# The gate half of an attention + gated MLP kernel: w_in's 512 columns read from two halves in turn

## Chip, cores and metric

The kernel runs on one core of one Trainium2 chip. The metric is the device time of one execution in microseconds (us); lower is better. Three runs of the kernel before gave 534.77, 535.20 and 535.42 us.

## What is computed

Attention with pooled keys and values feeds a gated MLP with a spatial gate. Cut to what matters:

```python
# attention: 8 batches, 8 heads, 576 positions, 64 wide; K and V averaged in groups of 8
x = softmax(q @ pool(k).T / 8) @ pool(v)         # (8, 576, 512)
h = gelu_tanh(x @ w_in)                          # w_in (512, 1024)
u, v = h[..., :512], h[..., 512:]                # v: the gate half
v_n = (v - mean(v)) / sqrt(var(v) + 1e-6) * g_ln
v_s = w_sg @ v_n + b_sg                          # over the 576 positions
out = x + (u * v_s) @ w_out                      # w_out (512, 512)
```

## The kernel before

Everything stays on the chip between the loads and the stores. Each batch passes through steps with one-letter names: loads of K, V and q (A, B, C, E), pooling (K, P), scores and softmax (S), moving the probabilities to the layout of the next product (L, T), the product with V (V), the gate half of w_in's product (H), the other half (U), the spatial gate (W), the last product (O) and the store (Z). For batch 0 alone the products of H for the first four position tiles stand in a step of their own, J, which goes through the contraction chunks as w_in arrives; D fills TensorE at the start. The order of all steps over all batches is one long table written out by hand, `ORDER`; a dependency chain at the end of the program keeps each engine in that order. Batches overlap: steps of batch b+1 and b+2 stand between those of batch b.

Products in 32 bits that must be exact are done as three products in the type fp32r: an operand is split into a high part that fp32r holds and the rest, and high x high, high x rest and rest x high are summed in PSUM. `wih` and `wil` are the two parts of w_in, 128 partitions by 4 contraction chunks by 1024 columns; columns 512 to 1023 (`DF2:2 * DF2`) are the gate half. `xhl` holds the two parts of x, and `xta` the last 64 positions of both.

Step H works by tiles of 128 positions, five to a batch (the last has 64). For a tile, x is the stationary operand (`lhsT`) and the 512 gate columns of one chunk are the moving operand (`rhs`): 4 chunks x 3 products for each full tile; in the last tile high and rest of x stand side by side as one stationary operand, 4 chunks x 2 products. That is 4 x 12 + 8 = 56 products of 512 columns for a batch, 448 for eight. All of them are issued by the helper `mm` in line 140. The result goes through Gelu (L668), its mean and variance (L672, L673), and the normalisation (L484 or L488), in which a position's 512 columns are read as one row, and is split again (`vhh`, `vhl`, `vht`) for step W, in which the columns pick the rows of the output: d-th group of 128 columns for the d-th part of u. So the columns must leave H in their order.

The other products have moving operands of 288 columns (half of 576 positions: steps U, W, O, V) or 144 (the scores, S, in plain 32 bits).

w_in is loaded as it lies in memory (`load_w`, four loads of 1 MB, in a 64-bit type) and made into `wih` and `wil` by `step_w`: L276 and L279 on ScalarE (ACT) take the upper and the lower word of each 64-bit value, words that lie 8 bytes apart in `raw`; L278 and L281 put them together, and L220/L222 and L225 split them. Sums of eight neighbours on GpSimd (POOL) are in `sum8`: L360 adds the first and second half of each group of eight, then of each four; L361 adds elements 0 and 1 of each group, which lie 32 bytes apart from group to group.

Of the kernel before, what the change touches and what calls it, by code (L numbers as in the profile page):

```python
# [95 lines left out]
def tile_pooled_attn_gmlp(ctx: ExitStack, tc: tile.TileContext, q, k0, kv0, v0, k, v, vleft, w_in, w_sg, bg, w_out, out):  # L96
# [5 lines left out]
    DF2 = w_in.shape[1] // 2  # L102
# [3 lines left out]
    KC = DM // P  # L106
# [21 lines left out]
    def ring(pool, shape, name, bufs):  # L128

        turns[name] = (turns.get(name, -1) + 1) % bufs  # L130
        return pool.tile(shape, F32, name=name, tag=f"{name}{turns[name]}")

    def mtile():
        return ring(psm, [P, 2, NB], "mps", 2)

    def atile():
        return ring(psa, [P, 2, NB], "aps", 2)

    def mm(o, lhsT, rhs, start, stop):
        nc.tensor.matmul(o, lhsT, rhs, start=start, stop=stop)  # L140
# [49 lines left out]
    wih = const.tile([P, KC, 2 * DF2], F32R, name="wih")  # L190
    wil = const.tile([P, KC, 2 * DF2], F32R, name="wil")
# [7 lines left out]
    both = const.tile([P, S + DF2 // P], F32, name="both")  # L199
# [6 lines left out]
    def ready(func):  # L206

        if loaded.get("now") != func:
            nc.scalar.activation(early, eps[:, 0:1], func)
        loaded["now"] = func  # L210

    def copy(o, i, key):
        if key in OTHER:
            nc.vector.tensor_copy(o, i)
        else:
            nc.scalar.copy(o, i)  # L216
# [7 lines left out]
    def combine(o, x, y, op, key):  # L224
        (nc.vector if key in OTHER else nc.gpsimd).tensor_tensor(o, x, y, op=op)  # L225
# [112 lines left out]
    def step_D(b, _):  # L338

        for _ in range(DRY):  # L340
            ps = atile()[:, 0, 0:P]
            for _ in range(2):
                mm(ps, ident, ident, True, True)
            yield
# [131 lines left out]
    def root(rstd, var, key):  # L476
        n = rstd.shape[0]
        nc.gpsimd.tensor_tensor(rstd, var, eps[:n, 1:2], op=ALU.add)  # L478
        nc.gpsimd.tensor_tensor(rstd, rstd, mhalf[:n], op=ALU.pow)

    def scaled(vg, mv, rstd, key):

        if key in OTHER:
            nc.vector.scalar_tensor_tensor(vg, vg, mv[:, 0:1], rstd.broadcast_to(list(vg.shape)),  # L484
                                           op0=ALU.subtract, op1=ALU.mult)
            return
        nc.gpsimd.tensor_scalar(mv[:, 0:1], mv[:, 0:1], rstd, -1.0, op0=ALU.mult, op1=ALU.mult)
        nc.scalar.activation(vg, vg, AF.Identity, bias=mv[:, 0:1], scale=rstd)  # L488

    def step_S(b, g):  # L490
        qT = st.pop(("qT", b, g))
        flat = (mtile() if (b, g) in BY_M else atile()).rearrange("p a n -> p (a n)")
        slots = []
        for i in range(NT):
# [63 lines left out]
    def step_T(b, g):  # L558
        ef = st.pop(("e", b, g))
        tags = (("ah", "al"), ("lt0", "lt1"))[g % 2]  # L560
        if b == 0:
            st["a", b, g] = []
            for h in range(2):
                ps = atile().rearrange("p a n -> p (a n)")
                turn(ps, lambda i: ef[:, i, SP * h:SP * h + SP])
                yield
                t = per.tile([SP, S], F32, name=tags[h], tag=tags[h])
                copy(t, ps[0:SP, 0:S], f"T{h}{g}")
                st["a", b, g].append(t)
                yield  # L570
            return
# [49 lines left out]
    def step_J(b, c):  # L621

        xhl = st["xhl", b][0]
        if c == 0:
            st["hp"] = [t[:, i] for t in (mtile(), mtile()) for i in range(2)]
        for pairs in (((wih, 0), (wih, 1)), ((wil, 0),)):
            for i, o in enumerate(st["hp"]):
                t = slice(i * P, i * P + P)
                for w, x in pairs:
                    mm(o, xhl[:, x, c, t], w[:, c, DF2:2 * DF2], c == 0 and w is wih and x == 0, c == KC - 1 and w is wil)  # L630
            yield

    def step_H(b, i):
        by_c = b == 0 and i < NT - 1
        if by_c:
            yield
        xhl, xta = st["xhl", b]
        xhi, xlo = xhl[:, 0], xhl[:, 1]
        o = st["hp"][i] if by_c else mtile()[:, 0]
        n = min(P, S - i * P)  # L640
        t = slice(i * P, i * P + n)
        sl = slice(DF2, 2 * DF2)
        for c in range(0 if by_c else KC):
            if i < NT - 1:
                mm(o, xhi[:, c, t], wih[:, c, sl], c == 0, False)
                mm(o, xhi[:, c, t], wil[:, c, sl], False, False)
                mm(o, xlo[:, c, t], wih[:, c, sl], False, c == KC - 1)
            else:

                both = (xta[:, c].rearrange("p a t -> p (a t)"), wih[:, c, sl], c == 0, c == KC - 1)  # L650
                if c == 0:
                    mm(o, *both)
                mm(o[:n], xta[:, c, 0], wil[:, c, sl], False, False)
                if c > 0:
                    mm(o, *both)
        if not by_c:
            yield
        vg = ring(per, [P, DF2], "vg", 3)[:n]
        if i == NT - 1:
            nc.scalar.copy(vg, o[n:2 * n])  # L660
            yield
            nc.vector.tensor_tensor(vg, o[:n], vg, op=ALU.add)
            yield
            ready(AF.Gelu_apprx_tanh)
            nc.scalar.activation(vg, vg, AF.Gelu_apprx_tanh)
        else:
            ready(AF.Gelu_apprx_tanh)
            nc.scalar.activation(vg, o, AF.Gelu_apprx_tanh)  # L668
        yield
        bst = per.tile([P, 6], F32, name="bst", tag=f"bst{i}")[:n]  # L670
        mv = per.tile([P, 2], F32, name="mv", tag=f"mv{i}")[:n]
        nc.vector.bn_stats(bst, vg)  # L672
        nc.vector.bn_aggr(mv, bst)  # L673
        rstd = per.tile([P, 1], F32, name="rstd", tag=f"rstd{i}")[:n]
        root(rstd, mv[:, 1:2], f"r{min(b, 3)}{i}")
        yield
        scaled(vg, mv, rstd, f"z{min(b, 3)}{i}")
        yield
        if ("vh", b) not in st:
            st["vh", b] = (per.tile([P, NT - 1, DF2], F32R, name="vhh", tag="vhhi"),  # L680
                           per.tile([P, NT - 1, DF2], F32R, name="vhl", tag="vhlo"),
                           per.tile([P, DF2], F32R, name="vht"))
        vhh, vhl, vht = st["vh", b]
        hi, lo = (vhh[:, i], vhl[:, i]) if i < NT - 1 else (vht[0:TAIL], vht[TAIL:2 * TAIL])
        copy(hi, vg, f"g{min(b, 2)}{i}")
        yield
        if i < NT - 1:
            combine(lo, vg, hi.bitcast(F32), ALU.subtract, f"H{min(b, 2)}{i}")
        else:
            nc.vector.tensor_tensor(lo, vg, hi.bitcast(F32), op=ALU.subtract)  # L690
# [127 lines left out]
def _laid_out(inputs):  # L818

    import numpy as np  # L820

    a = {n: np.asarray(x) for n, x in inputs.items()}
    B, H, S, D = a["q"].shape
    G, SP, NT = H // 2, S // POOL, -(-S // P)
    q = a["q"].reshape(B, G, 2, S, D).transpose(0, 1, 2, 4, 3).reshape(B, G, 2 * D, S)
    at = [128 * min(r, 2) + 160 * max(r - 2, 0) + 32 * i + j
          for i in range(NT) for r in range(2 * (i == NT - 1), 4) for j in range(32)]
    a["q"] = np.stack([q[b] if b == 0 else q[b][:, :, at] for b in range(B)])
    n = P * (S // P)
    run = [t for lo, hi in ((0, 384), (448, 576), (384, 448)) for t in range(lo, hi)]  # L830
    kt = a["k"][0].reshape(G, 2, S, D).transpose(2, 0, 1, 3).reshape(S, G, 2 * D)[run]
    vt = a["v"][0].reshape(G, 2, S, D).transpose(2, 1, 0, 3).reshape(S, H * D)[run]
    a["k0"] = kt[:n].reshape(S // P, P, G, 2 * D).transpose(1, 2, 0, 3)
    a["v0"] = vt[:n].reshape(S // P, P, H * D).transpose(1, 0, 2)
    a["kv0"] = np.concatenate([kt[n:].reshape(S - n, H * D), vt[n:]])
    a["k"] = a["k"][1:].reshape(B - 1, G, 2, SP, POOL, D).transpose(0, 2, 5, 1, 3, 4).reshape(B - 1, 2 * D, G, SP, POOL)
    v = a["v"][1:].reshape(B - 1, G, 2 * SP, POOL, D).transpose(0, 1, 2, 4, 3)
    a["v"] = v[:, :, 0:P].transpose(0, 2, 1, 3, 4)
    a["vleft"] = v[:, :, P:].reshape(B - 1, G * (2 * SP - P), D, POOL)
    a["moe_w_sg"] = np.concatenate([a["moe_w_sg"].T, a["moe_w_sg"].T[n:]])  # L840
    a["bg"] = np.concatenate([np.broadcast_to(a["moe_b_sg"], (P, S)), a["moe_g_ln"].reshape(-1, P).T], axis=1)
    return a
# [21 lines left out]
```

## Time and profile before

| | |
|---|---|
| median of three runs | 535.2 us (534.77 to 535.42) |
| profiled execution, span from the first to the last instruction | 534.0 us |
| TensorE (PE) busy | 525.2 us, 98% of the span |
| weight loads of TensorE (PEld) busy, beside PE | 489.6 us |
| VectorE (DVE) / ScalarE (ACT) / GpSimd (POOL) busy | 376.9 / 257.9 / 240.5 us |
| mean granted TensorE clock | 0.999 of 2.4 GHz |

Of the profiled execution only its span is given; the runs are timed apart from it, and their median lies 1.2 us above that span. Busy time of PE counts overlapping matmuls once. A matmul's own duration, from its start to its modelled end, is longer than the distance to the next one, since they are pipelined; what a matmul takes of the span is read from the distance of starts, for which the chain of work that ended last is the best view: it gives stretches with their number of matmuls.

### The profile page before, as it was taken

Reading aid. Unit: us, or ns where it says so; the run is one execution under the profiler, and the core shown is the slowest. Engines: PE = TensorE matmul, PEld = TensorE weight load, DVE = VectorE, ACT = ScalarE, POOL = GpSimd, SP = SyncE. Lnnn points to the kernel's source line nnn. Section 1 sums busy time; section 2 is a strip of 40 time slices with the busy share of each in tenths; the row PEclk is TensorE's granted clock in tenths of the full one; section 3 lists DMA queues with packets and bytes.
Section 4 is the critical chain, followed back from the end, with each engine's and each line's share of the span. In section 5 each row is a group of like instructions: output and inputs, shape, how many; then the busy total and the mean of one; then the engine's idle time right before and its main releaser. Section 6 shows DMA issues by size and latency. Waiting matters only on the chain.

```text
span 534.0 us, 9508 instructions
## 1 busy us (share of the span) xinstructions
PE 525.2 (98%) x3594; PEld 489.6 (92%) x3594; DVE 376.9 (71%) x593; ACT 257.9 (48%) x510; POOL 240.5 (45%) x333
## 2 busy tenths in 40 slices
PE   8889999999999999999999999999999999999997
PEld 8658999889989999898998999989999999999997
DVE  1788999668857886876679769877749765642362
ACT  2787871586336554475613567274253743142100
POOL 4797664553445628173325614754134641251010
PEclk9999999999999999999999999999999999999999
DMA  8995125837461563056432533344431224000002
GB/s 284 405 335 187 54 68 127 241 101 231 103 182 57 151 222 96 24 144 201 129 106 87 181 89 87 112 108 117 139 126 23 88 68 112 24 22 23 23 2 110
DMA packets 42810, 66.64 MB, mean 125 GB/s; under 512 B 5532, under 2 KB 22028, under 8 KB 42764
## 3 DMA queue, kind: packets, MB, share of 16 engines
q1 hardware_dynamic: 42476, 65.59, 40.3%
q8 instruction: 28, 0.46, 0.4%
q10 hardware_dynamic: 288, 0.44, 0.2%
q14 instruction: 18, 0.15, 0.1%
HBM read 47.14 MB, written 18.73 MB: 123 GB/s over the span
## 4 chain that ended last, share of the span: by engine, by line
PE 96%; ACT 2%; DVE 1%; POOL 0%; issue 0%; POOLq 0%; ACTq 0%
PE mps L140 80%; PE aps L140 15%; ACT e L469 1%; PE aps L187 0%; DVE nmax L503 0%; ACT ah L216 0%; ACT vg L668 0%; ACT xhl L216 0%; ACT raw L279 0%; ACT x L216 0%; DVE e L460 0%; ACT vg L488 0%; DVE bst L672 0%; DVE vhl L225 0%; ACT top L276 0%
## 5 line engine op out<-in xcount | busy, mean ns | idle before, releaser
L140 PE MATMUL mps<-xhl,wih 128*128 128x288 f32 x512 | 88.7, 294 | 0.1
L140 PE MATMUL mps<-wih,xhl 128*128 128x512 f32 x256 | 82.0, 398 | 0.0
L140 PEld LDWEIGHTS mps<-xhl,wih 128*128 128x128 f32 x512 | 75.2, 188 | 1.3 <-ACT vht L216 0.4
L455 POOL TENSOR_TENSOR e<-e,ssum 128x720 f32<-128x720 f32 x29 | 42.1, 1455 | 58.0 <-DVE ssum L454 53.5
L140 PEld LDWEIGHTS mps<-wih,xhl 128*128 128x128 f32 x256 | 47.8, 188 | 10.7
L232 POOL TENSOR_TENSOR xhl<-x,xhl 128x576 fp32r<-128x576 f32 x22 | 31.3, 1433 | 53.9 <-ACT x L216 34.6
L140 PE MATMUL mps<-wsh,vhh 128*128 128x288 f32 x256 | 54.8, 295 | 0.0
L140 PE MATMUL mps<-wsl,vhh 128*128 128x288 f32 x256 | 54.7, 295 | 0.0
L140 PE MATMUL mps<-wsh,vhl 128*128 128x288 f32 x256 | 54.7, 295 | 0.0
L140 PE MATMUL mps<-xhl,wil 128*128 128x288 f32 x256 | 54.6, 294 | 0.0
L140 PE MATMUL mps<-ghi,woh 128*128 128x288 f32 x244 | 53.1, 298 | 0.0
L140 PE MATMUL mps<-glo,woh 128*128 128x288 f32 x244 | 52.3, 294 | 0.0
L140 PE MATMUL mps<-ghi,wol 128*128 128x288 f32 x244 | 52.3, 294 | 0.0
L722 DVE SCALAR_TENSOR_TENSOR mps<-mps,both 128x576 f32<-128x576 f32 x32 | 26.1, 814 | 34.9 <-PE mps L140 34.6
L140 PE MATMUL mps<-wil,xhl 128*128 128x512 f32 x128 | 48.6, 395 | 0.0
L478 POOL TENSOR_TENSOR rstd<-mv,eps 128x1 f32<-128x1 f32 (+1 forms) x40 | 9.9, 247 | 80.3 <-DVE mv L673 79.9
L225 POOL TENSOR_TENSOR glo<-u,ghi 128x576 fp32r<-128x576 f32 x18 | 25.7, 1430 | 41.0 <-ACT ghi L216 23.9
L140 PEld LDWEIGHTS aps<-kbd,qT 128*128 128x128 f32 x300 | 39.0, 190 | 4.5 <-ACT ah L216 1.4
L140 PE MATMUL aps<-kbd,qT 128*128 128x144 f32 x300 | 41.6, 288 | 1.5 <-ACT ah L216 1.2
L760 DVE TENSOR_TENSOR x<-mps,x 128x576 f32<-128x576 f32 x30 | 22.4, 745 | 27.3 <-PE mps L140 27.2
L140 PEld LDWEIGHTS mps<-wsh,vhh 128*128 128x128 f32 x256 | 41.1, 188 | 0.4 <-issue 0.4
L140 PEld LDWEIGHTS mps<-wsh,vhl 128*128 128x128 f32 x256 | 41.1, 188 | 0.2 <-DVE vhl L225 0.2
(182 smaller groups left out, 1256.7 us busy)
## 6 DMA issues: line engine op xcount, KB each, us to landing
qT<-in_q SPq DMA_DIRECT2D x31, 288.0 KB
out<-x SPq DMA_DIRECT2D x31, 288.0 KB
kraw<-in_k SPq DMA_DIRECT2D x14, 576.0 KB
vraw<-in_v SPq DMA_DIRECT2D x14, 512.0 KB
al<-tfar SPq DMA_DIRECT2D x20, 288.0 KB
tfar<-y SPq DMA_DIRECT2D x56, 80.0 KB
raw<-in_moe_w_in SPq DMA_DIRECT2D x4, 1024.0 KB
tfar<-y SPq DMA_DIRECT2D x56, 64.0 KB
```

The lines of the kernel that those rows point to most:

```text
L140: nc.tensor.matmul(o, lhsT, rhs, start=start, stop=stop)
L225: (nc.vector if key in OTHER else nc.gpsimd).tensor_tensor(o, x, y, op=op)
L232: nc.gpsimd.tensor_tensor(lo, x, hi, op=ALU.subtract)
L455: (nc.gpsimd if key in OTHER else nc.vector).tensor_tensor(e, e, rec.unsqueeze(3).broadcast_to([P, NT, 2, SP]), op=ALU.mult)
L469: nc.scalar.activation(e[:, i, h], slots[i][:, h], AF.Exp, bias=nmax[:, i, h:h + 1], accum_out=ssum[:, i, h:h + 1])
L478: nc.gpsimd.tensor_tensor(rstd, var, eps[:n, 1:2], op=ALU.add)
L722: nc.vector.scalar_tensor_tensor(vs, vs, gcol[:, d:d + 1], bbc.rearrange("p (a n) -> p a n", a=2), op0=ALU.mult, op1=ALU.add)
L760: nc.vector.tensor_tensor(x, ps[:, :, 0:HALF], x, op=ALU.add)
```

## The change

The moving operand of every gate-half product is read by an access pattern that takes column 0 of the slice, column 256, column 1, column 257, and so on: 256 pairs whose two elements lie 256 columns (1024 bytes) apart. On the host the gate half of w_in is set out so that the even columns come first and the odd ones after them; read in that way, they come out in order. Loads, splits, number of products, number of columns and the order of issue on all engines are the same as before.

```diff
+    def woven(x):
+        return x.rearrange("p (a b) -> p b a", a=2)
+
...
                 for w, x in pairs:
-                    mm(o, xhl[:, x, c, t], w[:, c, DF2:2 * DF2], c == 0 and w is wih and x == 0, c == KC - 1 and w is wil)
+                    mm(o, xhl[:, x, c, t], woven(w[:, c, DF2:2 * DF2]), c == 0 and w is wih and x == 0, c == KC - 1 and w is wil)
...
             if i < NT - 1:
-                mm(o, xhi[:, c, t], wih[:, c, sl], c == 0, False)
-                mm(o, xhi[:, c, t], wil[:, c, sl], False, False)
-                mm(o, xlo[:, c, t], wih[:, c, sl], False, c == KC - 1)
+                mm(o, xhi[:, c, t], woven(wih[:, c, sl]), c == 0, False)
+                mm(o, xhi[:, c, t], woven(wil[:, c, sl]), False, False)
+                mm(o, xlo[:, c, t], woven(wih[:, c, sl]), False, c == KC - 1)
             else:
 
-                both = (xta[:, c].rearrange("p a t -> p (a t)"), wih[:, c, sl], c == 0, c == KC - 1)
+                both = (xta[:, c].rearrange("p a t -> p (a t)"), woven(wih[:, c, sl]), c == 0, c == KC - 1)
                 if c == 0:
                     mm(o, *both)
-                mm(o[:n], xta[:, c, 0], wil[:, c, sl], False, False)
+                mm(o[:n], xta[:, c, 0], woven(wil[:, c, sl]), False, False)
...
+    w = a["moe_w_in"]
+    half = w.shape[1] // 2
+    a["moe_w_in"] = np.concatenate([w[:, :half], w[:, half::2], w[:, half + 1::2]], axis=1)
```

## Rows read from the trace of the kernel before

**Rows 1.** The page's busy times, and the granted clock in its 40 slices.

```profile
PE 525.2 (98%) x3594; PEld 489.6 (92%) x3594; DVE 376.9 (71%) x593; ACT 257.9 (48%) x510; POOL 240.5 (45%) x333
...
PEclk9999999999999999999999999999999999999999
```

**Rows 2.** The chain that ended last, the page's shares by engine.

```profile
PE 96%; ACT 2%; DVE 1%; POOL 0%; issue 0%; POOLq 0%; ACTq 0%
```

**Rows 3.** Stretches: length, busy us (instructions) of each engine, clock, DMA share, GB/s.

```profile
0.00:36.00 36.00, 30.99 (x198) 25.10 (x199) 19.87 (x33) 21.75 (x53) 24.80 (x44) 1.00 0.98 346
36.00:56.50 20.50, 20.20 (x111) 15.99 (x108) 17.72 (x31) 17.39 (x48) 14.42 (x18) 1.00 0.64 216
...
200.00:300.00 100.00, 99.99 (x691) 95.23 (x690) 75.92 (x117) 50.19 (x85) 47.92 (x62) 1.00 0.39 113
...
480.00:534.00 54.00, 50.64 (x368) 49.33 (x367) 20.55 (x33) 5.99 (x11) 4.94 (x7) 0.99 0.11 42
```

**Rows 4.** Gate-half matmuls, groups by line and shape: count, busy us, mean ns.

```profile
L140 PE MATMUL mps<-wih,xhl 128*128 128x512 f32 x256 | 82.0, 398 | 0.0
...
L140 PE MATMUL mps<-wil,xhl 128*128 128x512 f32 x128 | 48.6, 395 | 0.0
...
L140 PE MATMUL mps<-wih,xta 128*128 128x512 f32 x32 | 13.0, 406 | 0.0
...
L140 PE MATMUL mps<-wil,xta 128*64 128x512 f32 x32 | 11.2, 392 | 0.0
```

**Rows 5.** Chain in order of time: 24 gate-half matmuls, then 56 of step W.

```profile
113.10 5.60 PE mps L140 x24
...
447.72 7.40 PE mps L140 x56
```

**Rows 6.** The page's DMA issues: the loads of w_in and w_out.

```profile
raw<-in_moe_w_in SPq DMA_DIRECT2D x4, 1024.0 KB
```

**Rows 7.** Plain 32-bit matmuls, chain in time: batch 0's V pooling (512 columns), scores (144).

```profile
22.93 4.49 PE mps L140 x10
...
118.69 2.45 PE aps L140 x20
```

**Rows 8.** The same matmuls grouped by line and shape.

```profile
L140 PE MATMUL aps<-kbd,qT 128*128 128x144 f32 x300 | 41.6, 288 | 1.5 <-ACT ah L216 1.2 <-PE mps L140 0.2
...
L140 PE MATMUL mps<-raw,pool 128*128 128x512 f32 x8 | 3.6, 592 | 0.0
```

**Rows 9.** The stretch of batch 0's V pooling: PE busy, clock, DMA share, GB/s.

```profile
22.90:27.50 4.60, 4.60 (x13) 1.00 1.04 388
```

**Rows 10.** GpSimd, groups by line and shape: one-column operation, then sums of eight.

```profile
L478 POOL TENSOR_TENSOR rstd<-mv,eps 128x1 f32<-128x1 f32 x32 | 7.7, 241 | 61.5 <-DVE mv L673 61.1
...
L360 POOL TENSOR_TENSOR vraw<-vraw 128x512 f32<-128x512 f32 x5 | 7.0, 1395 | 12.7 <-DVE e L460 7.3 <-DMA vraw<-in_v 5.5
...
L361 POOL TENSOR_TENSOR vp<-vraw 128x128 f32<-128x128 f32 x5 | 2.3, 450 | 0.4
```

**Rows 11.** ScalarE, groups by line and shape: words 8 bytes apart, then adjacent.

```profile
L276 ACT ACTIVATE top<-raw 128x512 f32<-128x512 f32 x12 | 8.2, 682 | 3.5 <-DMA raw<-in_moe_w_in 1.7 <-POOL wil L225 1.7
L279 ACT ACTIVATE raw<-raw 128x512 int32<-128x512 uint32 x12 | 8.2, 680 | 0.0
...
L222 ACT CAST wih<-top 128x512 fp32r<-128x512 f32 x1 | 0.6, 617 | 0.0
```

## Prediction

> **What bounds the kernel now.** I read the page's busy times first. PE is busy 525.2 of 534.0 us [rows 1], and the chain of work that ended last is PE for 96% [rows 2]. The stretches then say where the other 8.8 us lie: 36.00 - 30.99 = 5.0 us before 36 us, 0.3 us from there to 56.5 us and 54.00 - 50.64 = 3.4 us in the last stretch; between 200 and 300 us PE lacks 0.01 us [rows 3]. So from 36 us on, where the first gate-half product stands, to the tail, PE is never let wait: what a matmul gains or loses there is gained or lost by the span, one for one. The groups by shape count the products that the change touches: 256 + 128 + 32 + 32 = 448, each of 512 columns [rows 4]. Their mean of 398 ns is not their price, because they overlap; the chain gives 24 of them in 5.60 us, **233.3 ns** from one to the next, 0.456 ns a column. Step W's 288 columns take 7.40 us / 56 = 132.1 ns, 0.459 ns a column [rows 5]. Both sizes pay by the column, hardly by the instruction: the columns' pace is what counts. At the granted clock, 2.4 GHz throughout [rows 1], a column at each clock would be 0.417 ns; the rows say 9 to 10% more.
>
> **The change, part by part.** The host's new order of columns lies outside the device time. The loads of w_in keep their number, sizes and runs [rows 6]; the splits work element by element and don't notice which column is which. Gelu and the normalisation get the columns in the old order. No instruction is added, taken out or moved on any queue, and no wait is added. All of that costs nothing because it is the same work.
>
> What is left is 448 products whose moving operand jumps 1024 bytes at every column. No matmul of the trace reads a moving operand that way: all others, too, read neighbouring columns. So its price must be bounded from other rows.
>
> - *Nothing.* POOL's L361 reads elements 32 bytes apart: 450 ns for 128, and with the 241 ns of a one-column operation taken off 1.63 ns an element. L360 reads runs of four: (1395 - 241) / 512 = 2.25 ns [rows 10]. Reading apart is no dearer there. But that engine takes an element in the time of four TensorE columns, and a memory that is slow only against 0.456 ns would not show.
> - *A tenth.* ACT's L276 and L279 read words 8 bytes apart, 682 and 680 ns for 512; the cast of neighbouring words takes 617 ns [rows 11]. Their functions differ, so the 64 ns is an upper bound for the step there. Added to each product it is 448 x 64 ns = 28.7 us.
> - *Half the pace.* Plain 32-bit products leave two records each (300 for 150 products of scores), and 20 of these of 144 columns take 2.45 us: 122.5 ns, 0.851 ns a column; the ten of V pooling, 512 columns, take 4.49 us, 449 ns each, with PE never idle and the clock at 1.00 [rows 7 to 9]. This is a pace of one column in two clocks, and the only slower pace at which this trace shows TensorE being fed. 512 columns at 0.851 ns are 435.6 ns; 435.6 - 233.3 = 202.3 ns, times 448 = **90.6 us**. With 449 ns it would be 96.6 us, and with twice 233.3 ns 104.5 us.
> - *A quarter of it.* If each column cost what POOL pays for an element that lies apart, 1.63 ns, a product would take 835 ns: 448 x (835 - 233) = 270 us.
>
> I take half the pace, 90.6 us. The reason is the nearest row: gate products already run 9% under one column a clock while reading neighbours, and plain 32-bit products, which ask for a column half as often, don't lose that (0.851 / 2 = 0.425 ns per feed against 0.456). Something on the read side, I infer, is already at its limit when four bytes are asked for at each clock. A pattern in which no two successive elements are neighbours can hardly relieve it, and if the memory delivers more than one element per access, it delivers one of use now.
>
> [...] By the POOL row alone the sum would be nothing.
>
> Nothing covers the 90.6 us, since PE waits nowhere in these stretches [rows 3]. Nothing new becomes late either: the other engines' work lies in PE's shadow and gets more time. At most the 0.3 us of waits between 36 and 56.5 us could vanish. The clock should hold, as it did while V pooling fed at half pace [rows 9]. Sum, against the profiled execution's span: 534.0 + 90.6 = 624.6 us; with the 1.2 us by which the median lies above that span, **626 us**.
>
> **The rivals.**
>
> *No change, 535 us.* If the reader keeps both places open, each jump lands in what it already holds: two streams, each of neighbours. Any read-ahead of two streams would do it. For it speaks POOL's row [rows 10], and that the two halves are regular. Against it speaks the pace that is already under the clock. That the change doesn't do what it says would give the same time; but the products remain one instruction each of 512 columns, and the columns are right only if the read alternates. [...]
>
> *A tenth slower, 564 us*: the 28.7 us above, if a jump costs a fraction of a column.
>
> *A quarter of the pace, about 800 us*: 534.0 + 270 + 1.2 = 805 us. The same would come out, near enough, if such a pattern put a product onto the plain 32-bit path with two records: 2 x 435.6 ns, 448 x 638 ns = 286 us, 821 us. Nothing in the trace speaks for either.
>
> *Faster, 528 us.* The mechanism is on the read side: if the 9% is lost because neighbouring columns come from one place in the memory that is busy with itself, taking two places in turn would let a product run at the feed of the plain ones, 0.425 ns a column: 218 ns, (218 - 233.3) x 448 = -6.9 us, 534.0 - 6.9 + 1.2 = 528 us. It decides from the point at which two distant reads overlap and two near ones don't. The gap between 0.456 and 0.425 ns [rows 5, 7] is what speaks for it; nothing says that distance closes it.
>
> **How the numbers follow.** Half the pace has 0.52, a tenth slower (anything from 1 to 15%) 0.08, a quarter of the pace 0.08, no change 0.27, faster 0.05. So slower by over 0.2% has 0.68, within 0.2% 0.27, faster 0.05; 0.2% is about what a measurement of this kernel can tell from no change. The prediction is that of half the pace, 626 us, whose own range is 620 to 643 us: from exactly two clocks of 0.417 ns a column, 512 x 0.833 = 427 ns, 448 x 193.4 = 86.6 us and 622 us, to twice 233.3 ns, 534.0 + 104.5 + 1.2 = 640 us, each with a little to spare. To hold 8 in 10 the range must take in no change as well: 533.5 to 643 us leaves out the quarter and the gain, 0.13.
>
> **What would show it.** Right: matmuls of 512 columns on `wih` and `wil` with a mean near 590 ns, as V pooling's 592 ns [rows 8]; 24 of them in about 10.5 us of the chain instead of 5.60 us; those of 288 columns still 132 ns apart; PE idle still near 9 us; clock 1.00. Wrong: 398 ns and 5.60 us unchanged (no change), 5.2 us (faster), or four times the distance. If the products keep 233 ns and the time still grows, the mistake is in the claim that nothing else moves; if they slow down and the time grows less than their sum, it is in the claim that PE has no slack.

## The result, and the profile after

The changed kernel takes 528.65 us (median of four runs, 528.11 to 529.36) against 535.31 us before (four runs, 534.77 to 537.72); the ratio is 0.9874, 95% interval 0.985 to 0.9899. It is **faster by 1.3%**, with the whole interval below 1, where the forecast said 626 us, slower, with 0.05 for faster. The profiled execution has a time of 528.84 us and a span of 527.1 us, 6.9 us less than before.

First the page's busy times and the granted clock, as in [rows 1]:

```profile
PE 517.7 (98%) x3594; PEld 489.9 (93%) x3594; DVE 376.2 (71%) x593; ACT 258.3 (49%) x510; POOL 240.7 (46%) x333
...
PEclk9999999999999999999999999999999999999999
```

The groups by line and shape, as in [rows 4] (line 140 is now line 143):

```profile
L143 PE MATMUL mps<-wih,xhl 128*128 128x512 f32 x256 | 77.7, 383 | 0.0
...
L143 PE MATMUL mps<-wil,xhl 128*128 128x512 f32 x128 | 46.5, 379 | 0.0
...
L143 PE MATMUL mps<-wih,xta 128*128 128x512 f32 x32 | 12.6, 393 | 0.0
...
L143 PE MATMUL mps<-wil,xta 128*64 128x512 f32 x32 | 10.8, 379 | 0.0
```

The chain in order of time, as in [rows 5]:

```profile
111.81 5.18 PE mps L143 x24
...
441.77 7.39 PE mps L143 x56
```

The chain's shares by engine, as in [rows 2]:

```profile
PE 92%; ACT 3%; DVE 2%; POOL 2%; issue 0%; POOLq 0%; ACTq 0%
```

And the stretches, as in [rows 3]:

```profile
0.00:36.00 36.00, 30.97 (x199) 25.09 (x200) 20.07 (x34) 22.00 (x53) 25.01 (x44) 1.00 0.97 346
36.00:56.50 20.50, 19.85 (x115) 16.69 (x114) 18.35 (x31) 18.49 (x49) 14.12 (x18) 1.00 0.64 216
...
200.00:300.00 100.00, 99.67 (x701) 96.54 (x700) 78.29 (x124) 48.09 (x82) 49.77 (x65) 1.00 0.40 117
473.00:527.10 54.10, 50.79 (x372) 49.81 (x370) 20.98 (x33) 6.60 (x11) 5.86 (x8) 0.99 0.12 45
```

24 gate-half products take 5.18 us instead of 5.60 us: **215.8 ns** from one to the next instead of 233.3 ns. Step W's products of 288 columns, which the change doesn't touch, stay at 7.39 us / 56 = 132 ns. 448 x 17.5 ns = 7.8 us; the span gives 6.9 us of it. Of the 0.9 us between them 0.6 us is in PE's waits: 527.1 - 517.7 = 9.4 us idle instead of 8.8 us, such as 20.50 - 19.85 = 0.65 us instead of 0.3 us in the second stretch. The other 0.3 us is not traced: PE's busy time fell by 525.2 - 517.7 = 7.5 us. The other engines' work has a little less cover, and here and there it is now late.

At 0.417 ns a column, the prediction's one a clock, 512 columns are 213.3 ns. So the changed product runs at that pace with 2.5 ns over, and the question is what neighbours cost: 17.5 ns for 512 columns. Two sizes show the pace: step W's products of 288 columns, read in two groups in turn in a run further down, are 122.5 ns apart, and (215.8 - 122.5) / 224 is 0.417 ns a column, 2.4 columns a ns.

### The profile page after: what moved, and what is told of

Same layout as the page of the kernel before. It is cut to its first block, busy times and chain, and to the rows that moved or that the text cites. A ratio compares the mean times of both kernels' runs of the same rounds, so it can differ in the third digit from the quotient of the medians.

```text
span 527.1 us, 9508 instructions
## 1 busy us (share of the span) xinstructions
PE 517.7 (98%) x3594; PEld 489.9 (93%) x3594; DVE 376.2 (71%) x593; ACT 258.3 (49%) x510; POOL 240.7 (46%) x333
## 4 chain that ended last, share of the span: by engine, by line
PE 92%; ACT 3%; DVE 2%; POOL 2%; issue 0%; POOLq 0%; ACTq 0%
PE mps L143 77%; PE aps L143 15%; ACT e L472 1%; POOL e L458 1%; DVE nmax L506 0%; PE aps L190 0%; POOL rstd L482 0%; DVE e L463 0%; ACT vg L491 0%; DVE glo L228 0%; ACT e L468 0%; POOL glo L228 0%; ACT ah L219 0%; ACT L212 0%; ACT vhh L219 0%
## 5 line engine op out<-in xcount | busy, mean ns | idle before, releaser
L143 PE MATMUL mps<-wih,xhl 128*128 128x512 f32 x256 | 77.7, 383 | 0.0
L143 PE MATMUL mps<-wil,xhl 128*128 128x512 f32 x128 | 46.5, 379 | 0.0
L143 PEld LDWEIGHTS mps<-xhl,wil 128*128 128x128 f32 x256 | 40.9, 188 | 0.0
```

## The experiments

For ten of the kernels below there is one time each, beside 535.82 us of the kernel before (535.02 us for the orders of four places and of two neighbours from each half); what decides in each is the distance of the gate-half products in the chain, which is alike to 0.02 us in all its stretches. In the gate-half experiments only the pattern of `woven` is changed, and on the host the columns are set out so that they come out in order:

```diff
-    a["moe_w_in"] = np.concatenate([w[:, :half], w[:, half::2], w[:, half + 1::2]], axis=1)
+    at = ...
+    a["moe_w_in"] = w.copy()
+    a["moe_w_in"][:, half + at] = w[:, half:]
```

where `at` is the order in which the pattern reads.

### Four orders

**Runs of 128 from the two halves in turn.**

```diff
-        return x.rearrange("p (a b) -> p b a", a=2)
+        return x.rearrange("p (a b r) -> p b a r", a=2, r=128)
```

> Same pattern form as the change (more than one free dimension), but runs of 128 neighbouring columns taken from the two halves in turn. Theory A (two distant places in turn relieve a read that is at its limit): nearly every successor is a neighbour, so 233 ns a gate product and about 535 us. Theory B (a successor in another group of four columns, 16 bytes, relieves it) and theory C (any successor that isn't the next column): also 233 ns, 535 us. Theory D (the form of the pattern, not the addresses, changes how the operand is fetched): 216 ns and about 528.6 us.

**Two adjacent groups of four in turn.**

```diff
-        return x.rearrange("p (a b) -> p b a", a=2)
+        return x.rearrange("p (k a b) -> p k b a", a=2, b=4)
```

> Columns of two adjacent groups of four in turn: 0, 4, 1, 5, 2, 6, 3, 7, then the next eight; successors lie 16 or 12 bytes apart instead of 1024. Theory A: the places are not distant, so 233 ns a gate product, 535 us. Theories B, C and D: 216 ns, about 528.6 us.

**Every fourth column.**

```diff
-        return x.rearrange("p (a b) -> p b a", a=2)
+        return x.rearrange("p (a b) -> p b a", b=4)
```

> Every fourth column in turn, 16 bytes from one to the next, four passes over the 2 KB: one stream, and no group of four gives two successors. Theory A: one place that moves on, 233 ns, 535 us. Theories B, C and D: 216 ns, 528.6 us. The theory of the forecast (an access delivers only one element of use, half the pace) would have 427 to 467 ns and 620 to 640 us; the change has already refuted it for two streams, and here there is only one.

**Another order within each group of four.**

```diff
-        return x.rearrange("p (a b) -> p b a", a=2)
+        return x.rearrange("p (k a b) -> p k b a", a=2, b=2)
```

> The order within each group of four columns is 0, 2, 1, 3; the group is left only after its four. Theories A and B: 233 ns a gate product, 535 us. Theories C and D: 216 ns, 528.6 us.

The chain in order of time, 24 gate-half products, of runs of 128 (536.58 us):

```profile
112.87 5.60 PE mps L143 x24
```

of two adjacent groups in turn (529.11 us):

```profile
112.25 5.18 PE mps L143 x24
```

of every fourth column (636.64 us):

```profile
130.11 11.07 PE mps L143 x24
```

and of the order 0, 2, 1, 3 within each group (536.88 us):

```profile
114.24 5.60 PE mps L143 x24
```

That is 233.3, 215.8, 461 and 233.3 ns. The form of the pattern does nothing (runs of 128, 233.3 ns: theory D falls). The distance of the two places does nothing either: 215.8 ns at 16 bytes as at 1024 (theory A falls). That successors aren't neighbours is not enough (0, 2, 1, 3, in which three of four successors aren't, is as slow as neighbours, and every fourth column is twice as slow: theory C falls). Theory B has three of four right and misses the fourth by a factor of two: in steps of 16 bytes each successor lies in another group, and the product takes 461 ns, **the half pace of the forecast**: 448 x (461 - 233) ns = 102 us, measured 636.64 - 535.82 = 101 us. Read in the terms of the forecast: one stream that leaves a group after each column does pay about 0.9 ns a column (461 / 512), and the change, which leaves a group after each column too but comes back to it, doesn't (215.8 ns).

### What must be used of a group, and when

**Every second column.**

```diff
-        return x.rearrange("p (a b) -> p b a", a=2)
+        return x.rearrange("p (a b) -> p b a", b=2)
```

> Every second column, then the others (0, 2, 4, ..., 510, 1, 3, ...): one stream, 8 bytes from one to the next, so that each group of four columns gives two and is left, and comes again in the second pass. Theory E (the earlier looks: a group fetched takes 0.9 ns, the 461 ns for 512 of a 16-byte step; neighbours are slow because a new group is only asked for when the old one is used up): two columns to a fetch, 0.45 ns a column, 231 to 235 ns a gate product, about 535 to 537 us. Theory F (half of the successors lie in another group, and that is what relieves it): 216 to 225 ns, 528.6 to 532 us.

**Two halves in turn, two columns of a group in a pass.**

```diff
-        return x.rearrange("p (a b) -> p b a", a=2)
+        return x.rearrange("p (a b c) -> p c b a", a=2, c=2)
```

> Two places 1024 bytes apart in turn as in the change, but each group of four columns gives only two (0, 256, 2, 258, then the next groups; the odd ones in a second pass). Theory E as a limit on fetches (0.9 ns each): two columns to a fetch, 0.45 ns a column, 231 to 235 ns, about 535 to 537 us. Theory F (every successor in another group): 216 ns, 528.6 us.

**Eight columns in the order 0, 2, 4, 6, 1, 3, 5, 7.**

```diff
-        return x.rearrange("p (a b) -> p b a", a=2)
+        return x.rearrange("p (k b a) -> p k a b", b=4, a=2)
```

> Within eight neighbouring columns the order 0, 2, 4, 6, 1, 3, 5, 7: two from one group of four, two from the next, two from the first again, two from the second; all four columns of a group are used within seven. Theory E: four columns to a fetch and the second group asked for early, 216 ns, 528.6 us. Theory F: half of the successors in another group, between 216 and 225 ns. If every successor must lie in another group: 233 ns, 535 us.

The same row of the chain, of every second column (632.67 us):

```profile
129.19 10.87 PE mps L143 x24
```

of two halves with two columns in a pass (539.17 us):

```profile
116.79 5.60 PE mps L143 x24
```

and of the order 0, 2, 4, 6, 1, 3, 5, 7 (581.76 us):

```profile
119.92 8.15 PE mps L143 x24
```

453, 233.3 and 340 ns. Theories E and F as they were put both fall: E has only the second of the three, F none. Every second column and two halves with two columns in a pass both take two columns of a group and leave it, and yet one is at half pace and the other as good as neighbours. Two columns of a group in a pass can't be the whole measure: it matters **which** two follow one another. (The second kernel's 539.17 us is 3 us more than its products explain; its granted clock was 0.92 in the first 36 us, where the kernel before had 1.00 [rows 3].) The stretch shows that:

```profile
0.00:36.00 36.00, 31.32 (x185) 25.89 (x185) 19.59 (x32) 20.42 (x50) 23.72 (x42) 0.92 0.97 344
```

What fits best is theory G, a supposition of mine, worked out from the distances measured above; no run shows a lane or a fetch. Call the columns at even positions of the read one lane, and those at odd positions the other. The theory supposes that a lane pays whenever it goes to another group of four columns (16 bytes), one such fetch at a time. In the step of 16 bytes each lane changes its group at each of its columns: (461.3 - 2.5) / 512 = 0.896 ns a column, two lanes, so by estimate 1.79 ns a fetch. From that one number, the 0.417 ns a column and the 2.5 ns a product that are over (215.8 - 213.3, from the change itself) the theory estimates:

| order read | columns of a lane in a row from one group | estimate by theory G, ns | measured, ns |
|---|---|---|---|
| neighbours; runs of 128; 0, 2, 1, 3; two halves, two columns in a pass | 2 | 512 x 1.79 / 4 + 2.5 = 232 | 233.3 in all four |
| two halves; two adjacent groups | 4 | 512 x 1.79 / 8 is under 512 x 0.417, so 512 x 0.417 + 2.5 = 216 | 215.8 in both |
| every second column | 1 | 461 | 453 |
| 0, 2, 4, 6, 1, 3, 5, 7 | 1 | 461 | 340, which does not fit |

The group of four is itself read from these rows. With groups of two, neighbours would change the group at every column of a lane, as every second column does, yet the two stand at 233.3 and 453 ns; with groups of eight, two adjacent groups of four would be no better than neighbours, yet they stand at 215.8 ns.

### Two further orders for theory G

**Four places in turn.**

```diff
-        return x.rearrange("p (a b) -> p b a", a=2)
+        return x.rearrange("p (a b) -> p b a", a=4)
```

> Gate half alone: four places 512 bytes apart in turn (0, 128, 256, 384, 1, 129, ...). Theory G (lanes): TensorE takes the columns of even position and those of odd position by two lanes; each lane fetches a group of four columns in about 1.8 ns (two lanes of 0.9 ns a column in the 16-byte step) and keeps it until it needs another; neighbours give a lane two columns to a fetch, the change four. Here a lane changes its group at each column, places 0 and 2 in the one, 1 and 3 in the other: slow, 453 to 461 ns a gate product and about 632 to 637 us if a lane keeps one group, less if it keeps two (340 ns as in the order 0, 2, 4, 6, 1, 3, 5, 7). Theory F (every successor in another group, all four columns of a group used while they are at hand): 216 ns, 529 us.

**Two neighbours from each half in turn.**

```diff
-        return x.rearrange("p (a b) -> p b a", a=2)
+        return x.rearrange("p (a b r) -> p b a r", a=2, r=2)
```

> Gate half alone: two neighbours from each half in turn (0, 1, 256, 257, 2, 3, 258, 259). Theory G: the even lane gets 0, 256, 2, 258, the odd lane 1, 257, 3, 259, so both change their group at each column: 340 to 461 ns, 582 to 637 us, although each pair of columns is neighbours. Theory F: every second successor in another group, four columns used of each within seven: 216 to 225 ns, 529 to 533 us.

The chain's row for four places (556.40 us):

```profile
116.46 6.79 PE mps L143 x24
```

and for two neighbours from each half (576.39 us):

```profile
118.87 7.84 PE mps L143 x24
```

283 and 327 ns: both slower than plain neighbours, as theory G has it and theory F excludes, but both below the sizes that theory G gave beforehand (340 to 461 ns); G has the direction and misses the size. The second is the telling one. It reads the same two places as the change, uses all of a group's columns within six, and has neighbours in every pair; only the length of the run differs, two instead of one. With runs of two each lane sees both places in turn and changes its group at each column. But neither number, nor the 340 ns above, is the 453 to 461 ns that theory G has for a lane that keeps one group only. If a lane kept two, the theory would have four places at the change's 216 ns, and the other two orders at the 233 ns of neighbours; the three are 67, 94 and 107 ns slower than that. **Open** is what sets these three distances; and that a lane fetches at all is supposed, no run shows it.

What holds for all eleven orders, neighbours and the change with them, is the sorting. Take the columns at even positions of the read, and those at odd positions, each as a row of their own, and count how many follow one another out of one group of four: four gave 215.8 ns (two orders), two gave 233.3 ns (four orders), one gave 283 to 461 ns (five orders). Nine of the eleven were known when theory G was thought of; the last two were run to test them and fell on the slow side.

### The same for other products

**The change, and step W in turn between adjacent groups of four.**

```diff
+    def near(x):
+        return x.rearrange("p (k a b) -> p k b a", a=2, b=4)
...
-                mm(ps[:, n, 0:HALF], w, x[:, HALF * n:HALF * (n + 1)], first and j == 0, last and j == len(pairs) - 1)
+                mm(ps[:, n, 0:HALF], w, by(x[:, HALF * n:HALF * (n + 1)]), first and j == 0, last and j == len(pairs) - 1)
```

Step W passes `near` as `by`; the columns of w_sg are set out on the host as above.

> The change, and in step W the same done to w_sg: its 896 products of 288 columns read two adjacent groups of four in turn, with the columns set out on the host. If a column's extra 0.034 ns belongs to reading neighbours and not to the gate products, each falls from 132.1 to 288 x 0.417 + 2.5 = 122.5 ns: 896 x 9.6 = 8.6 us less, about 520 us. If a product of 288 columns is held by the loading of its weights, it stays at 132 ns and 528.7 us.

It takes 523.17 us. The chain, 56 products of step W and 24 gate-half products:

```profile
111.92 5.18 PE mps L146 x24
...
438.32 6.86 PE mps L146 x56
```

6.86 us / 56 = 122.5 ns instead of 132 ns, to the tenth what was expected: the loss belongs to reading neighbours in fp32r, not to the gate products or to the loading of weights. 5.5 us of the 8.6 us arrive, so the time is 523 us and not the expected 520. PE now waits for others in the middle of the program: from 36 to 473 us it lacks 437.00 - 434.09 = 2.9 us, where with the change alone it lacks 1.0 us. The two stretches, of the change and of this run:

```profile
36.00:473.00 437.00, 435.96 (x3027) 415.00 (x3026) 335.10 (x528) 229.69 (x447) 209.83 (x283) 1.00 0.40 118
36.00:473.00 437.00, 434.09 (x3056) 412.49 (x3056) 338.42 (x530) 231.14 (x449) 210.39 (x284) 1.00 0.41 119
```

The chain's shares by engine show it too:

```profile
PE 82%; DVE 8%; ACT 4%; POOL 4%; DMA 1%; issue 1%; SPq 0%; POOLq 0%; ACTq 0%
```

**Steps U, W and O as well.**

```diff
...
-                   c == 0, c == KC - 1)
+                   c == 0, c == KC - 1, near)
...
-        nc.vector.tensor_tensor(x, ps[:, :, 0:HALF], x, op=ALU.add)
+        y = x.rearrange("p n (k b a) -> p n k a b", b=4, a=2)
+        nc.vector.tensor_tensor(y, ps[:, :, 0:HALF].rearrange("p n (k a b) -> p n k a b", a=2, b=4), y, op=ALU.add)
...
-    a["bg"] = np.concatenate([np.broadcast_to(a["moe_b_sg"], (P, S)), a["moe_g_ln"].reshape(-1, P).T], axis=1)
+    a["bg"] = np.concatenate([np.broadcast_to(a["moe_b_sg"][at], (P, S)), a["moe_g_ln"].reshape(-1, P).T], axis=1)
```

The first edit stands in U and O alike, W has `near` as in the run before, and O's other form, in which x is added in parts, has the same two edits; w_sg is again as before, and its columns come out in the order that U gives u.

> The change, and in steps U, W and O, too, the moving operand is read from two adjacent groups of four in turn (0, 4, 1, 5, 2, 6, 3, 7): 768 + 896 + 768 products of 288 columns. U leaves its columns in that order, W makes its own agree (w_sg as it lies, the bias set out on the host), O permutes once more, and DVE's addition of x reads and writes x by the pattern that undoes it. By theory G each of the 2432 products falls from 132.1 to 122.5 ns, 23.3 us; W alone gave 5.5 of its 8.6 us, because waits on DVE and POOL came up, so I expect 508 to 514 us where the sum says 505. If the waits eat all that U and O give: 523 us. If the addition in steps of 8 bytes costs DVE much, the product tiles come free late and it is slower than 523 us.

Here there are four times: **513.16 us** (512.64 to 515.63) against 535.02 us, ratio 0.9593, interval 0.9552 to 0.9634, within the expected 508 to 514 us. It beats both kernels. The chain, step U's and step W's products:

```profile
186.88 5.88 PE mps L149 x48
193.83 6.86 PE mps L149 x56
```

The addition of x, the group by line and shape, in the kernel before and here:

```profile
L760 DVE TENSOR_TENSOR x<-mps,x 128x576 f32<-128x576 f32 x30 | 22.4, 745 | 27.3 <-PE mps L140 27.2
...
L771 DVE TENSOR_TENSOR x<-mps,x 128x576 f32<-128x576 f32 x30 | 22.3, 744 | 18.9 <-PE mps L149 18.8
```

and the chain's shares by engine:

```profile
PE 69%; DVE 13%; ACT 6%; POOL 5%; DMA 3%; issue 2%; SPq 1%; POOLq 0%; ACTq 0%; DVEq 0%
```

U and W run at 122.5 ns a product. The addition that puts the columns back in steps of 8 bytes takes 744 ns in the mean, where the plain one of the kernel before took 745 ns: it costs nothing. Of the 23.3 us beside the change, 528.65 - 513.16 = 15.5 us arrive. The chain now runs through DVE for 13% and PE for 69%, from 96% [rows 2]: TensorE is still busy for 497.7 of 510.9 us, but the kernel no longer waits for TensorE alone.

## Why the prediction was wrong, step by step

- **What bounds the kernel**: right. PE had no slack, and what the products gained became the span's but for 0.9 us. That nothing else moves and that the clock holds was right too, but for the 0.6 us of new waits: the page has the same 3594 matmuls, at a mean granted clock of 0.999 as before.
- **"Half the pace"**, the term of 90.6 us, is the step that failed. In its place the runs show 17.5 ns less a product, -7.8 us for the 448. What went wrong in it is the sentence that "a pattern in which no two successive elements are neighbours can hardly relieve" a read at its limit, delivering "one of use" per access. The pace itself was sized well: every fourth column, one stream that leaves its group after each column, takes 461 ns and 101 us more, near the upper price of 104.5 us. But the two halves in turn are not that order. Each of the two streams walks through neighbours, and that takes 215.8 ns. I priced the jump from one column to the next, and not what each of the two streams still takes in a row from the place that it is in. "One of use" per access was my supposition; no run shows what an access delivers.
- **The inference before it** was right: of the 9% over 0.417 ns a column all but 2.5 ns a product was lost on the read side, since the order of reading alone brought it back (233.3 to 215.8 ns), and the plain products of the scores, at 0.851 ns a column, don't lose it (0.851 / 2 = 0.425 ns). It should have weighed for the rival "faster", which used the same gap.
- **The rival "faster, 528 us"** has the number: 218 ns and -6.9 us, where 215.8 ns, 7.8 us for the products and 6.9 us for the span were measured. Its place, "one place in the memory that is busy with itself", fell with the adjacent groups: 215.8 ns at 16 bytes as at 1024. What replaces it, as far as the distances show, is how many columns in a row the even and the odd positions each take from one group of four. Its point of decision, "two distant reads overlap and two near ones don't", was the wrong one.
- **The rival "no change"** was right that going to the other half at every column costs nothing (215.8 ns); that the reader keeps both open was its supposition, and no run shows it. It missed that reading neighbours is itself slower (233.3 ns).

## What to carry to other kernels

Where TensorE bounds a kernel and its fp32r products of neighbouring columns run, as here, some 9% over 0.417 ns a column, read the moving operand from two groups of four columns in turn (0, 4, 1, 5, 2, 6, 3, 7, or two halves), and set the columns out on the host or let a later read undo it: each product of 512 columns gave 17.5 ns here, each of 288 gave 9.6 ns. Runs of two from two halves, four places or steps of 8 or 16 bytes were slower than neighbours here, up to twice, so such a pattern is to be measured by the distance of the products before it is used. When a read's price is asked, don't count the jumps, and don't count either what a place gives in all: four places in turn use every column of a group and still take 283 ns. Count, for the even and the odd positions apart, how many columns in a row come from one group.

## What was not expected of the hardware

- Reading neighbours is not the fastest way: 233.3 ns for 512 columns against 215.8 ns from two groups in turn, with all else equal.
- A step of 8 bytes costs as much as one of 16 (453 and 461 ns), though it uses two columns of each group of four; taken from two halves in turn, two columns of a group in a pass cost as neighbours do (233.3 ns).
- Two neighbours from each of two places in turn take 327 ns, half as much again as one from each.
- On DVE an addition that reads and writes x in steps of 8 bytes takes 744 ns, no longer than the plain one.
